# Agent attention and feed-forward: source order on four engines inside the main loop, and the attention work spread over single steps

## The chip, the cores and the metric

The kernel runs on one core of one Trainium2 chip. The metric is the device time of one launch in microseconds (us), the median of several executions. The core has five engines that run side by side and meet only at semaphores: PE (matrix multiplication; its weight loads are shown as PEld), DVE (elementwise work and reductions), ACT (activation functions and copies), POOL (elementwise work in SBUF) and SP, which here only issues DMAs. Each engine runs its own instructions in the order in which the program lists them.

## The reference, cut to what matters

```python
B, N, C, A = 4, 12480, 128, 49          # batches, tokens, width, agents
def sm(a, b):
    s = scale * (a @ b.transpose(0, 2, 1))
    s = s - s.max(-1, keepdims=True)
    e = np.exp(s)
    return e / (e.sum(-1, keepdims=True) + 1e-09)
agent_v = sm(agents, k) @ v             # per batch, 49 x 128
attn    = sm(q, agents) @ agent_v       # per batch, 12480 x 128
h = attn.reshape(49920, 128) @ w_in     # to 2048 hidden values
out = (h / (1 + np.exp(-1.702 * h))) @ w_out
```

A batch's queries need the sums over all of that batch's keys and values. All is float32 in the reference; `w_in` and `w_out` come as float64.

## The kernel before, in words

**Tiling.** A group is 960 tokens; a batch has 13 groups, and there are 52 in all. The 2048 hidden values of a group are computed in 16 steps of 128, so the main loop (L540 to L569) has 832 steps. `agent_v` is never multiplied with the query weights by itself: it is first multiplied into `w_in` (L306), once a batch, and the product is kept as a high part `wh` and a low part `wl` in float32r (L307, L308).

**A step.** `up` (L357) makes four matmuls of 128 x 480 columns into two of the four PSUM buffers `ph`, then ACT takes the gelu of both (L369, output `g`, three buffers), then `gh`, g rounded to float32r, is made on ACT (L371) for the steps listed in `HI_ON_ACT` and on DVE (L373) for the others, then DVE makes the rest `gl = g - gh` (L374). Both have `LAG + 1` = 5 buffers. `down` (L377) of the step four earlier makes six matmuls into the group's output `po`. After a group's last `down`, `store` copies `po` on ACT (L396) and SP sends it.

**Beside it**, for the next group: the query load (SP), `split` of the queries into three bfloat16 parts (POOL, L167 to L169), 32 small matmuls for the scores with the agents (`scores`, L182 to L185, two of the two PSUM buffers `ps_m`) whose two banks DVE reduces (L189), the softmax (DVE max and subtraction, L321 and L322; ACT exp, L328; DVE sum, reciprocal and product, L330 to L334), and four transposes with two ACT copies and two DVE subtractions that give the pairs `sa`, `sb` on which the next group's `up` works (L345 to L353).

**For the next batch**, spread over the 13 groups of this one: 13 key chunks in groups 0 to 5 (1 to 5 in batch 0): load, `split` on POOL, the same 32 matmuls, two reductions and a maximum (L225). Then `key_max` (L229): a DVE maximum, a PE transpose (L235), two DVE instructions, a second transpose (L241), a DVE copy. Then 13 value chunks in groups 6 to 11: the shift by the maximum on POOL (L251), exp on ACT (L255), the high and low parts of the weights on ACT and POOL (L260, L261) and of the values on DVE (L267, L268), eight matmuls (L272), and the sum on DVE (L287). In group 12 `agent_weights` (L289) makes `wh` and `wl` for the next batch. In batch 0's group 0, steps 1, 5 and 9, there is `down_weights` (L142) besides: eight DVE instructions that turn a quarter of `w_out` from float64 words to float32 (`to_float32`, L124 to L136), an ACT copy (L145) and a DVE subtraction (L146). The words, the keys and the values share three buffers `kv`; `rest` of `split` and the temporary of `to_float32` share two.

**What sets the order.** The source puts these jobs at steps of the group (`beside`, L509, and the constants of L27 to L35): at a step, jobs first, then `up`, then `down`. The source's order isn't the program's: the framework's scheduler puts the instructions of every engine in an order of its own. It works through them by priority (earlier source first) against modelled times, and where one isn't ready it takes a later one. So one engine's order can leave the source's order, matmul by matmul. Once it is compiled the order is fixed.

Of the kernel before, what the change touches and what calls it, by code (L numbers as in the profile page):

```python
# [27 lines left out]
E_AT = 4  # L28
S_AT = 0
V_AT = 7  # L30
VP = 2
VS = 4
P_AT = 12
QS_AT = 11
K_AT = 5  # L35
FIRST_WORDS = (1, 3, 5, 7)
FIRST_UP = (0, 2, 4, 6)
HI_ON_ACT = (0, 2, 4, 6, 8, 10, 12, 14)
# [4 lines left out]
def kernel(  # L43
# [36 lines left out]
    # sel[k, m] = 1 where k and m name the same agent in either half  # L80
# [28 lines left out]
    # a float64's words, low then high, to the nearest float32; what is under  # L109
    # float32's range becomes zero and what is over it infinite  # L110
# [5 lines left out]
    def to_float32(w, out=None):  # L116
# [4 lines left out]
        # 2 ** exponent, with the sign  # L121
# [6 lines left out]
        # the mantissa's upper 45 bits as a whole number, rounded once  # L128
# [19 lines left out]
    # ---- scores: a float32 is the sum of three bfloat16, and of the parts'  # L148
    # products all are summed but those under a float32 product's own rounding ----
# [13 lines left out]
    # the upper half of a word is the first part; of what is left the upper  # L163
    # half is the second, and the third takes the place of the lower
# [35 lines left out]
    def first_key_scores(g, kt):  # L200
        # two batches' agents to a pass, as many columns as keep the clock up
# [20 lines left out]
    def key_scores(b, g, parts):  # L222
        s = score[:TB, g * KB : (g + 1) * KB, :]
        scores(b, parts, s)
        nc.vector.tensor_reduce(  # L225
            out=part_max[:TB, g, :], in_=s.rearrange("p j a -> p a j"), axis=AX.X, op=ALU.max
        )

    def key_max():  # L229
# [3 lines left out]
        )  # L233
        ps = ps_m.tile([P, 512], F32, name="ps_m")
# [4 lines left out]
        nc.vector.tensor_copy(out=mrow[:A], in_=mcol[:A].broadcast_to([A, TB]))  # L239
        ps = ps_m.tile([P, 512], F32, name="ps_m")  # L240
        nc.tensor.transpose(out=ps[:TB, :A], in_=mrow[:A], identity=ident[:A, :A])  # L241
        nc.vector.tensor_copy(out=max_b[:TB], in_=ps[:TB, :A])

# [19 lines left out]
    def value_pair(g, vt, hi_copy, parts=1):  # L263
        vp = v_pair[g % 2]
        n = KB // parts
        for s in [slice(i * n, (i + 1) * n) for i in range(parts)]:
            hi_copy(out=vp[:TB, s, 0:C], in_=vt[:TB, s])  # L267
            nc.vector.tensor_sub(out=vp[:TB, s, C : 2 * C], in0=vt[:TB, s], in1=vp[:TB, s, 0:C].bitcast(F32))  # L268
# [11 lines left out]
    def key_values(g, vt, acc):  # L280
        value_pair(g, vt, nc.vector.tensor_copy)
        ps = ps_m.tile([P, 512], F32, name="ps_m")
        key_matmuls(g, ps, True, True)
        if g == 0:
# [4 lines left out]
    def agent_weights(acc):  # L289
        ps = ps_m.tile([P, 512], F32, name="ps_m")  # L290
        nc.tensor.matmul(out=ps[:, 0:P], lhsT=acc[:, 0:C], rhs=sel, start=True, stop=False)
        nc.tensor.matmul(out=ps[:, 0:P], lhsT=acc[:, C : 2 * C], rhs=sel, start=False, stop=True)
        zc = work.tile([P, P], F32, name="zc", bufs=1)
        nc.vector.tensor_copy(out=zc, in_=acc[:, 2 * C : 2 * C + 1].broadcast_to([P, P]))
# [6 lines left out]
        wh = wpool.tile([P, F], F32R, name="wh")  # L301
        wl = wpool.tile([P, F], F32R, name="wl")
        for c in range(F // 512):
            s = slice(c * 512, (c + 1) * 512)
            pw = ps_m.tile([P, 512], F32, name="ps_m")
            nc.tensor.matmul(out=pw, lhsT=avT, rhs=w_in_sb[:, s], start=True, stop=True)  # L306
            nc.scalar.copy(out=wh[:, s], in_=pw)  # L307
            nc.vector.tensor_sub(out=wl[:, s], in0=pw, in1=wh[:, s].bitcast(F32))  # L308
        return wh, wl

# [6 lines left out]
    def query_shift(b, parts):  # L317
        sd = work.tile([P, KB, A], F32, name="sd", bufs=SD)
        scores(b, parts, sd[:TB])
        m = work.tile([P, KB], F32, name="m")  # L320
# [4 lines left out]
        return sd  # L325

    def query_softmax(g, e):
        nc.scalar.activation(out=e[:TB], in_=e[:TB], func=AF.Exp, scale=scale)  # L328
        z = work.tile([P, KB], F32, name="z")
        nc.vector.tensor_reduce(out=z[:TB], in_=e[:TB], axis=AX.X, op=ALU.add)  # L330
        nc.vector.tensor_scalar_add(out=z[:TB], in0=z[:TB], scalar1=EPS)
        nc.vector.reciprocal(out=z[:TB], in_=z[:TB])
        pp = p_pad[g % 2]
# [23 lines left out]
    def up(f, wts, pairs):  # L357
# [7 lines left out]
        g = gpool.tile([P, 2, CH], F32, name="g")  # L365
        gh = gpool.tile([P, 2, CH], F32R, name="gh", bufs=LAG + 1)
        gl = gpool.tile([P, 2, CH], F32R, name="gl", bufs=LAG + 1)
        for c in range(2):
            nc.scalar.activation(out=g[:, c, :], in_=ph[c][:, :CH], func=AF.Gelu_apprx_sigmoid)  # L369
# [36 lines left out]
    shifted = {}  # L406
# [26 lines left out]
    def do_key_values(b, g):  # L433
        if g == 0:
            accs[b] = work.tile([P, 2 * C + 1], F32, name="acc")
        key_values(g, vts.pop((b, g)), accs[b])

    def do_query_scores(n):
        if n < B * NG:
            b, g = divmod(n, NG)  # L440
            shifted[n] = query_shift(b, q_parts.pop(n))

    def do_query_softmax(n):
        if n < B * NG:
            query_softmax(n, shifted.pop(n))
# [5 lines left out]
    def do_weights(b):  # L451
        wts[b] = agent_weights(accs.pop(b))
# [28 lines left out]
    do_query_scores(0)  # L481
    do_query_softmax(0)
# [22 lines left out]
    do_weights(0)  # L505
    down_weights(0, words[0])

    # what is done for the next batch beside a group: in steps of the group's
    def beside(b, g):  # L509
        jobs = {}  # L510
        if b == 0 and g == 0:
            for i in range(1, NF // 4):
                jobs.setdefault(4 * i - 3, []).append(lambda i=i: down_weights(i, words[i]))
        if b + 1 < B:
            late = 1 if b == 0 else 0
            ks = [k for k in range(NKG) if late + k * (6 - late) // NKG == g]
            vs = [k for k in range(NKG) if k * 6 // NKG == g - 6]
            for i, k in enumerate(ks):
                jobs.setdefault(0, []).append(lambda k=k: do_key_load(b + 1, k))
                jobs.setdefault(4 * i, []).append(lambda k=k: do_key_split(b + 1, k))  # L520
                jobs.setdefault(K_AT + 4 * i, []).append(lambda k=k: do_key_scores(b + 1, k))
            if g == 5:
                jobs.setdefault(15, []).append(key_max)
            if vs:
                assert S_AT < E_AT < V_AT - VP
                jobs.setdefault(E_AT, []).append(lambda: key_exp(vs[0], len(vs)))
            for i, k in enumerate(vs):
                jobs.setdefault(0, []).append(lambda k=k: do_value_load(b + 1, k))
                jobs.setdefault(S_AT, []).append(lambda k=k: key_shift(k, nc.gpsimd.tensor_tensor))
                jobs.setdefault(V_AT - VP + VS * i, []).append(lambda k=k: key_pair(k))  # L530
                jobs.setdefault(V_AT + VS * i, []).append(lambda k=k: do_key_values(b + 1, k))
            if g == NG - 1:
                jobs.setdefault(2, []).append(lambda: do_weights(b + 1))
        assert all(f < NF for f in jobs)
        return jobs

    steps = B * NG * NF
    live = {}
    po = {}
    for t in range(steps + LAG):  # L540
        n, f = divmod(t, NF)
        if t < steps:
            b, g = divmod(n, NG)
            if f == 0:
                jobs = beside(b, g)
            if f == 0:
                do_query_load(n + 2)
                if n == 0:
                    do_query_split(1)
            if f == QS_AT:  # L550
                do_query_split(n + 2)
            if f == Q_AT:
                do_query_scores(n + 1)
            if f == E_AT:
                do_query_softmax(n + 1)
            for job in jobs.get(f, ()):
                job()
            if f == P_AT:
                do_query_pairs(n + 1)
            live[t] = up(f, wts[b], pairs[n])  # L560
            if f == NF - 1:
                pairs.pop(n)
        if t >= LAG:
            n, f = divmod(t - LAG, NF)
            if f == 0:
                po[n] = [ps_o.tile([P, 512], F32, name=f"po{c}") for c in range(2)]
            down(f, live.pop(t - LAG), po[n])
            if f == NF - 1:
                store(*divmod(n, NG), po.pop(n))  # L569
# [38 lines left out]
```

## Time and profile before

| | us |
|---|---|
| median of 3 runs (lowest, highest) | 2137.14 (2136.03, 2139.71) |
| the profiled execution, span from first to last instruction | 2139.6 |
| first matmul of the main loop | 73.00 |
| start of group 13, of group 26, of group 39 (batches 1, 2, 3) | 610.75, 1133.19, 1654.86 |
| mean granted TensorE clock | 0.992 of full speed |

The execution that was profiled is thus 2.5 us over the median; what lies outside its span isn't shown. The profile's page gives the busy time of each engine. A matmul's end is modelled and matmuls overlap, so PE busy isn't PE at its peak; it shows where PE had nothing to do. The windows view gives the same in stretches of time that one chooses: length, then busy us of each engine with the number of instructions, then the share of the clock that was granted to TensorE. The waits view says which engine's instruction ended the waits of another.

### The profile page before, as it was taken

The page shows a single profiled execution, that of the slowest core. Times are in us where ns is not written, and L with a number is a line of the kernel's source. Part 1 is how long each engine was busy: PE and PEld are TensorE (multiplying, and loading weights), DVE is VectorE, ACT ScalarE, POOL GpSimd, SP SyncE. Part 2 cuts the span into 40 slices and gives each one's busy share as a digit, 9 for nine tenths or more (in the row PEclk, how much of TensorE's full clock was granted, in tenths as well). Part 3 has the DMA queues.
Part 4 walks back from the last instruction along what each step waited for, and adds up shares of the span by engine and source line. Part 5 has one row for each costly group of instructions (what it writes and reads, how often), then busy time and mean ns, then how long its engine had stood idle before and what let it go on. Part 6 is the DMA issues. An engine that isn't in the chain of part 4 may idle for free.

```text
span 2139.6 us, 31613 instructions
## 1 busy us (share of the span) xinstructions
PE 2083.2 (97%) x12232; PEld 1777.1 (83%) x12232; DVE 1865.0 (87%) x2142; ACT 1611.9 (75%) x2590; POOL 519.8 (24%) x383
## 2 busy tenths in 40 slices
PE   8889989999999999999999999999999999999999
PEld 8678878888888887788888888778888888888887
DVE  6998998999889899899888899899898887888876
ACT  3567768977777776987777777798777877778786
POOL 4143445121123433421113342531110101001000
PEclk9999999999999999999999999999999999999999
DMA  9411221211111212112101212111100101010000
GB/s 265 119 48 49 65 73 38 61 48 50 38 38 47 66 47 56 47 56 56 56 20 47 63 49 56 55 51 53 47 19 19 38 19 38 19 38 20 25 14 19
DMA packets 49339, 108.57 MB, mean 51 GB/s; under 512 B 4252, under 2 KB 30172, under 8 KB 49188
## 3 DMA queue, kind: packets, MB, share of 16 engines
q1 hardware_dynamic: 49188, 106.55, 17.2%
q8 instruction: 96, 1.57, 0.3%
q14 instruction: 55, 0.45, 0.1%
HBM read 80.97 MB, written 25.56 MB: 50 GB/s over the span
## 4 chain that ended last, share of the span: by engine, by line
PE 81%; DVE 11%; issue 3%; ACT 3%; POOL 1%; DMA 1%; ACTq 0%; SPq 0%; DVEq 0%; POOLq 0%
PE po L385 43%; PE ph L362 15%; PE ph L364 14%; DVE gl L374 5%; DVE gh L373 2%; PE ps_m L272 1%; PE ps_m L182 1%; PE ps_m L184 1%; POOL score L251 1%; PE ps_m L205 1%; ACT g L369 1%; PE ps_m L345 1%; PE ps_m L306 1%; PE ps_m L183 1%; PE ps_m L185 1%
## 5 line engine op out<-in xcount | busy, mean ns | idle before, releaser
L374 DVE TENSOR_TENSOR gl<-g,gh 128x960 fp32r<-128x960 f32 x832 | 1034.4, 1258 | 189.4 <-ACT gh L371 174.3
L369 ACT ACTIVATE g<-ph 128x480 f32<-128x480 f32 x1664 | 855.2, 573 | 380.5 <-PE ph L364 265.7
L385 PE MATMUL po<-gl,wo_h 128*128 128x480 f32 x1664 | 501.9, 382 | 5.4 <-DVE gl L374 5.4
L385 PE MATMUL po<-gh,wo_h 128*128 128x480 f32 x1664 | 506.1, 383 | 0.7 <-ACT gh L371 0.7
L385 PE MATMUL po<-gh,wo_l 128*128 128x480 f32 x1664 | 501.6, 383 | 0.0
L371 ACT CAST gh<-g 128x960 fp32r<-128x960 f32 x416 | 416.0, 1000 | 10.9
L385 PEld LDWEIGHTS po<-gl,wo_h 128*128 128x128 f32 x1664 | 313.1, 189 | 60.0 <-DVE gl L374 9.2
L385 PEld LDWEIGHTS po<-gh,wo_h 128*128 128x128 f32 x1664 | 313.5, 189 | 53.2 <-ACT gh L371 1.1
L385 PEld LDWEIGHTS po<-gh,wo_l 128*128 128x128 f32 x1664 | 313.8, 189 | 49.9
L362 PE MATMUL ph<-sa,wh 128*128 128x480 f32 x832 | 332.5, 400 | 4.8 <-ACT g L369 4.8
L364 PE MATMUL ph<-sa,wl 128*128 128x480 f32 x832 | 319.3, 384 | 0.0
L362 PE MATMUL ph<-sb,wh 128*128 128x480 f32 x832 | 318.8, 383 | 0.0
L364 PE MATMUL ph<-sb,wl 128*128 128x480 f32 x832 | 316.6, 381 | 0.0
L373 DVE CAST gh<-g 128x960 fp32r<-128x960 f32 x416 | 298.6, 718 | 7.0 <-ACT g L369 6.6
L167 POOL MEMSET qt<- 128x8 f32 x52 | 5.7, 110 | 939.2 <-PE ps_m L185 472.0
L169 POOL TENSOR_TENSOR rest<-rest 128x968 bf16<-128x968 f32 x91 | 188.6, 2072 | 7.1
L362 PEld LDWEIGHTS ph<-sa,wh 128*128 128x128 f32 x832 | 157.7, 190 | 31.7 <-ACT g L369 10.8
L362 PEld LDWEIGHTS ph<-sb,wh 128*128 128x128 f32 x832 | 158.0, 190 | 26.6 <-ACT g L369 6.2
L364 PEld LDWEIGHTS ph<-sb,wl 128*128 128x128 f32 x832 | 156.9, 189 | 25.6 <-issue 1.0
L364 PEld LDWEIGHTS ph<-sa,wl 128*128 128x128 f32 x832 | 157.1, 189 | 24.7 <-issue 1.0
L168 POOL TENSOR_TENSOR rest<-qt 128x968 f32<-128x968 f32 x52 | 110.7, 2129 | 167.8 <-DMA qt<-qT 110.8
L184 PE MATMUL ps_m<-ag_part,rest 128*128 128x98 bf16 x728 | 110.2, 205 | 0.0
(103 smaller groups left out, 2077.8 us busy)
## 6 DMA issues: line engine op xcount, KB each, us to landing
kt<-kT SPq DMA_DIRECT2D x52, 480.0 KB, 3.6
qt<-qT SPq DMA_DIRECT2D x52, 480.0 KB, 3.8
vt<-v SPq DMA_DIRECT2D x52, 480.0 KB, 4.3
outT<-o SPq DMA_DIRECT2D x104, 240.0 KB, 2.2
words<-w_in SPq DMA_DIRECT2D x4, 512.0 KB, 10.9
words<-w_out SPq DMA_DIRECT2D x4, 512.0 KB, 8.2
ag_sb<-agT SPq DMA_DIRECT2D x1, 98.0 KB, 2.1
```

The source lines that it names most:

```text
L168: nc.gpsimd.tensor_sub(out=r, in0=t, in1=halves(t)[0])
L169: nc.gpsimd.tensor_sub(out=halves(r)[1], in0=r, in1=halves(r)[0])
L182: mm(out=o, lhsT=x0[:, t], rhs=a[:, 0 : 2 * A], start=True, stop=False)
L183: mm(out=o[:, A:], lhsT=x0[:, t], rhs=a[:, 2 * A :], start=False, stop=False)
L184: mm(out=o, lhsT=x1[:, t], rhs=a[:, 0 : 2 * A], start=False, stop=False)
L362: nc.tensor.matmul(out=ph[c][:, :CH], lhsT=wh[:, s], rhs=pairs[c], start=True, stop=False)
L364: nc.tensor.matmul(out=ph[c][:, :CH], lhsT=wl[:, s], rhs=pairs[c], start=False, stop=True)
L369: nc.scalar.activation(out=g[:, c, :], in_=ph[c][:, :CH], func=AF.Gelu_apprx_sigmoid)
L371: nc.scalar.copy(out=gh, in_=g)
L373: nc.vector.tensor_copy(out=gh, in_=g)
L374: nc.vector.tensor_sub(out=gl, in0=g, in1=gh.bitcast(F32))
L385: nc.tensor.matmul(out=po[c][:, :CH], lhsT=lhsT[:, f, :], rhs=rhs[:, c, :], start=(f == 0 and first), stop=(f == NF - 1 and last),)
```

## The change

Four things are done together.

1. The loop stands in `tc.manual_schedule(engines={PE, Activation, DVE, Pool})`: inside it these four engines take their instructions in the order of the source. SP isn't among them.
2. A step's order in the source becomes `up` with its two gelus, then the step's jobs, then `gh` and `gl` (the new `high_low`), then `down` of four steps earlier. Before, the jobs stood ahead of `up`, and `gh` and `gl` were part of it.
3. The jobs are cut into pieces, and each has a step. `key_scores` loses its maximum (`key_part_max`, a step later), `key_max` becomes three pieces (DVE; a transpose and two DVE instructions; a transpose and a DVE copy), `key_values` becomes the values' high part and low part, the matmuls, and the sum, at two steps before, one before, the step, and one after. The softmax is cut into shift, exp, sums and product. `agent_weights` becomes `weights_sums` and four `weights_part`, a step each. Steps on which PE has a job are given out by `pe_step`, which takes the next step that has none; each group's steps 4 (query scores) and 13 (query pairs) are taken from the start. Key chunks stand 6 steps apart in batch 0 (from step 16 of the batch) and 7 in the others (from step 6), value chunks 7 apart.
4. Constants: the exp of the queries moves from step 4 to step 7, and the key chunks' exps are put straight behind it, up to three chunks in one instruction, so that both use the exp table while it is loaded. The pairs move from step 12 to 13, the query split from 11 to 14, the query load from 0 to 5. `HI_ON_ACT` still has eight steps of 16, with 5 and 13 in place of 4 and 8.

The work is otherwise the same: each engine has the same instructions on the same operands, apart from the exps that are put together. The diff, cut to its core:

```diff
-E_AT = 4
-P_AT = 12
-QS_AT = 11
+E_AT = 7
+P_AT = 13
+S_AT = 14
-HI_ON_ACT = (0, 2, 4, 6, 8, 10, 12, 14)
+HI_ON_ACT = (0, 2, 5, 6, 10, 12, 13, 14)
...
+    for i in range(1, NF // 4):
+        put(4 * i - 3, lambda i=i: down_weights(i, words[i]))
+    put(0, lambda: do_query_split(1))
+    for b in range(B - 1):
+        s0 = b * per_batch
+        first, apart = (16, 6) if b == 0 else (6, 7)
+        for k in range(NKG):
+            t = pe_step(s0 + first + apart * k)
+            put(max(t - 13, s0), lambda b=b, k=k: do_key_load(b + 1, k))
+            put(max(t - 6, s0), lambda b=b, k=k: do_key_split(b + 1, k))
+            put(t, lambda b=b, k=k: do_key_scores(b + 1, k))
+            put(t + 1, lambda k=k: key_part_max(k))
+        mx = {}
+        put(t + 2, lambda mx=mx: key_max_0(mx))
+        t = pe_step(t + 3)
+        put(t, lambda mx=mx: key_max_1(mx))
+        t = pe_step(t + 2)
+        put(t, lambda mx=mx: key_max_2(mx))
+        shift = t + 2
+        slot = next(t for t in range(shift + 3, steps) if t % NF == E_AT)
+        t = slot + 3
+        for k in range(NKG):
+            t = pe_step(t)
+            while t > slot + NF + 5:
+                slot += NF
+            exps.setdefault(slot, []).append(k)
+            put(min(shift + 3 * k, slot - 1), lambda k=k: key_shift(k, nc.gpsimd.tensor_tensor))
+            put(t - 14, lambda b=b, k=k: do_value_load(b + 1, k))
+            put(t - 2, lambda k=k: key_pair(k))
+            put(t - 2, lambda b=b, k=k: value_hi(k, vts[b + 1, k]))
+            put(t - 1, lambda b=b, k=k: value_lo(k, vts.pop((b + 1, k))))
+            put(t, lambda b=b, k=k: do_key_values(b + 1, k))
+            put(t + 1, lambda b=b, k=k: do_key_sum(b + 1, k))
+            last, t = t, t + 7
+        put(pe_step(last + 2), lambda b=b, w=w: weights_sums(accs.pop(b + 1), w))
+        t = last + 3
+        for c in range(F // 512):
+            t = pe_step(t + 1)
+            put(t, lambda b=b, w=w, c=c: weights_part(b + 1, w, c))
+    for n in range(B * NG):
+        s0 = n * NF
+        put(s0 + Q_AT, lambda n=n: do_query_scores(n + 1))
+        put(s0 + Q_AT + 1, lambda n=n: do_query_load(n + 2))
+        put(s0 + Q_AT + 1, lambda n=n: do_query_shift(n + 1))
+        put(s0 + E_AT, lambda n=n: do_query_exp(n + 1))
+        if s0 + E_AT in exps:
+            put(s0 + E_AT, lambda ks=ks: key_exp(ks[0], len(ks)))
+        put(s0 + E_AT + 2, lambda n=n: do_query_sums(n + 1))
+        put(s0 + E_AT + 3, lambda n=n: do_query_softmax(n + 1))
+        put(s0 + P_AT, lambda n=n: do_query_pairs(n + 1))
+        put(s0 + S_AT, lambda n=n: do_query_split(n + 2))
...
+    with tc.manual_schedule(engines={E.PE, E.Activation, E.DVE, E.Pool}):
+        for t in range(steps + LAG):
+            if t < steps:
+                n, f = divmod(t, NF)
+                g = up(f, wts[n // NG], pairs[n])
...
+            for job in at.pop(t, ()):
+                job()
+            if t < steps:
+                live[t] = high_low(f, g)
+            if t >= LAG:
...
+                down(f, live.pop(t - LAG), po[n])
```

More of the change, by code (lines that the diff above doesn't have):

```diff
@@ L227, in key_scores, with key_max_0 @@
         )
-    def key_max():
+    def key_max_0(d):
         mx = work.tile([P, A], F32, name="mx", bufs=1)
@@ L239, in key_max, with key_max_2 @@
         nc.vector.tensor_copy(out=mrow[:A], in_=mcol[:A].broadcast_to([A, TB]))
+        d["mrow"] = mrow
+    def key_max_2(d):
+        mrow = d["mrow"]
         ps = ps_m.tile([P, 512], F32, name="ps_m")
@@ L242, in key_max @@
         nc.vector.tensor_copy(out=max_b[:TB], in_=ps[:TB, :A])
+    def key_max():
+        d = {}
+        key_max_0(d)
+        key_max_1(d)
+        key_max_2(d)
     def value_load(b, g):
@@ L261, in key_pair, with value_hi, value_lo @@
         nc.gpsimd.tensor_sub(out=ep[:TB, :, H : H + A], in0=sc, in1=ep[:TB, :, 0:A].bitcast(F32))
-    def value_pair(g, vt, hi_copy, parts=1):
+    def value_hi(g, vt):
+        nc.vector.tensor_copy(out=v_pair[g % 2][:TB, :, 0:C], in_=vt[:TB])
+    def value_lo(g, vt):
         vp = v_pair[g % 2]
[L265 to L268, printed above, removed]
+        nc.vector.tensor_sub(out=vp[:TB, :, C : 2 * C], in0=vt[:TB], in1=vp[:TB, :, 0:C].bitcast(F32))
     def key_matmuls(g, ps, first, last):
@@ L300, in agent_weights, with weights_part @@
         nc.vector.tensor_mul(out=avT, in0=ps[:, 0:P], in1=rz)
[L301 to L309, printed above, removed]
+        w["avT"] = avT
+    def weights_part(b, w, c):
+        if c == 0:
+            wts[b] = wpool.tile([P, F], F32R, name="wh"), wpool.tile([P, F], F32R, name="wl")
+        wh, wl = wts[b]
+        s = slice(c * 512, (c + 1) * 512)
+        pw = ps_m.tile([P, 512], F32, name="ps_m")
+        nc.tensor.matmul(out=pw, lhsT=w["avT"], rhs=w_in_sb[:, s], start=True, stop=True)
+        nc.scalar.copy(out=wh[:, s], in_=pw)
+        nc.vector.tensor_sub(out=wl[:, s], in0=pw, in1=wh[:, s].bitcast(F32))
     def query_load(b, g):
@@ L315, in query_load, with query_scores, query_shift @@
         return t
-    def query_shift(b, parts):
+    def query_scores(b, parts):
         sd = work.tile([P, KB, A], F32, name="sd", bufs=SD)
         scores(b, parts, sd[:TB])
+        return sd
+    def query_shift(sd):
         m = work.tile([P, KB], F32, name="m")
@@ L365, in up, with high_low @@
         g = gpool.tile([P, 2, CH], F32, name="g")
+        for c in range(2):
+            nc.scalar.activation(out=g[:, c, :], in_=ph[c][:, :CH], func=AF.Gelu_apprx_sigmoid)
+        return g
+    def high_low(f, g):
         gh = gpool.tile([P, 2, CH], F32R, name="gh", bufs=LAG + 1)
         gl = gpool.tile([P, 2, CH], F32R, name="gl", bufs=LAG + 1)
-        for c in range(2):
-            nc.scalar.activation(out=g[:, c, :], in_=ph[c][:, :CH], func=AF.Gelu_apprx_sigmoid)
         if f in HI_ON_ACT:
@@ L405 @@
     q_parts = {}
-    shifted = {}
+    scored = {}
+    sums = {}
     accs = {}
@@ L504 @@
     do_query_load(1)
-    do_weights(0)
+    w0 = {}
+    weights_sums(accs.pop(0), w0)
+    for c in range(F // 512):
+        weights_part(0, w0, c)
     down_weights(0, words[0])
[L509 to L535, printed above, removed]
@@ L538 @@
+    E = mybir.EngineType
     live = {}
     po = {}
[L540 to L556, printed above, removed]
-                job()
[L558 to L569, printed above, removed]
+    with tc.manual_schedule(engines={E.PE, E.Activation, E.DVE, E.Pool}):
[3 more added lines that the diff above has]
+                g = up(f, wts[n // NG], pairs[n])
+                if f == NF - 1:
+                    pairs.pop(n)
+            for job in at.pop(t, ()):
+                job()
+            if t < steps:
+                live[t] = high_low(f, g)
+            if t >= LAG:
+                n, f = divmod(t - LAG, NF)
+                if f == 0:
+                    po[n] = [ps_o.tile([P, 512], F32, name=f"po{c}") for c in range(2)]
+                down(f, live.pop(t - LAG), po[n])
+                if f == NF - 1:
+                    store(*divmod(n, NG), po.pop(n))
@@ L573 @@
+    assert not at
 _INS = ["qT", "kT", "v", "agT", "w_in", "w_out"]
```

64 lines of the change are left out of this document (47 added, 17 removed).

## The prediction

> **What bounds the kernel now.** I read the page first, then the windows by batch and by group, then PE's waits.
>
> ```profile
> span 2139.6 us, 31613 instructions
> PE 2083.2 (97%) x12232; PEld 1777.1 (83%) x12232; DVE 1865.0 (87%) x2142; ACT 1611.9 (75%) x2590; POOL 519.8 (24%) x383
> ```
>
> PE has work for 97% of the span. The windows by batch are cut at the first `up` matmul of groups 0, 13, 26, 39 and 51 (columns: length, then busy us of PE, PEld, DVE, ACT, POOL, then the granted clock):
>
> ```profile
> core 0: us, PE busy (x) PEld busy (x) DVE busy (x) ACT busy (x) POOL busy (x), PEclk, DMA share, GB/s
> 73.00:610.75 537.75, 517.72 (x3067) 437.38 (x3065) 488.77 (x561) 407.44 (x649) 157.60 (x109) 0.99 0.17 50
> 610.75:1133.19 522.44, 514.42 (x3085) 438.43 (x3084) 471.17 (x533) 404.17 (x644) 148.25 (x104) 0.99 0.17 50
> 1133.19:1654.86 521.67, 513.45 (x3086) 438.10 (x3085) 470.33 (x533) 404.43 (x644) 150.29 (x101) 1.00 0.16 47
> 1654.86:2095.03 440.17, 440.17 (x2353) 376.00 (x2352) 359.49 (x409) 350.25 (x564) 37.58 (x30) 1.00 0.08 25
> ```
>
> In the last row PE never stops: twelve groups with query work alone take 440.17, so 36.68 each. That is PE's own pace, and no order can beat it. Now single groups, cut the same way:
>
> ```profile
> 73.00:113.00 40.00, 36.15 (x194) 28.21 (x193) 39.27 (x59) 30.00 (x49) 11.99 (x8) 0.98 0.17 50
> 113.00:161.58 48.58, 42.58 (x278) 34.87 (x276) 47.23 (x48) 31.13 (x51) 18.60 (x13) 0.96 0.18 52
> 161.58:203.48 41.90, 40.43 (x293) 34.70 (x292) 38.15 (x43) 29.54 (x47) 18.25 (x12) 1.00 0.20 60
> 492.45:531.00 38.55, 38.55 (x214) 33.47 (x213) 35.74 (x43) 30.18 (x49) 6.90 (x7) 1.00 0.17 51
> 569.60:610.75 41.15, 41.15 (x212) 33.25 (x210) 34.39 (x42) 31.67 (x51) 3.90 (x3) 1.00 0.08 25
> 652.78:691.82 39.04, 39.04 (x261) 33.56 (x260) 35.91 (x42) 29.43 (x47) 13.52 (x9) 1.00 0.17 51
> 808.99:853.30 44.31, 40.89 (x263) 34.48 (x262) 43.69 (x50) 29.73 (x49) 15.10 (x9) 0.95 0.20 56
> 853.30:897.74 44.44, 41.93 (x221) 35.20 (x220) 37.42 (x39) 38.16 (x58) 25.95 (x19) 0.97 0.17 45
> ```
>
> Three of these also run without a PE gap and give the price of the jobs to PE: two key chunks 39.04 - 36.68, so 1.18 each; two value chunks 38.55 - 36.68, so 0.94 each; the weights 41.15 - 36.68 = 4.47. A batch that prepares the next one therefore costs PE at least 13 x 36.68 + 13 x 1.18 + 13 x 0.94 + 4.47, and about 0.3 for the two transposes of `key_max` (an estimate by the 0.30 of a row below): 509.2. The three batches took 537.75, 522.44 and 521.67: **28.6, 13.2 and 12.5 too much, 54.3 in all**. This is what another order can win. It sits in few groups. In batch 1: `key_max` (808.99, two chunks: 44.31 against 39.3) and the first value group (853.30, three chunks: 44.44 against 39.5) hold ten of the 13.2. Batch 0 has the like, and group 1 (113.00, three chunks: 48.58 against 40.2), 8.4 over. The waits of PE, summed over the run, name who is late:
>
> ```profile
> PE ps_m L182 <- DVE sb L353: 10.2, 5, 3.9
> PE ps_m L241 <- DVE mrow L239: 7.6, 3, 3.5
> PE po L385 <- DVE gl L374: 5.4, 9, 2.1
> PE ph L362 <- ACT g L369: 4.8, 6, 1.6
> PE ps_m L182 <- DVE sd L189: 4.5, 2, 4.2
> PE ps_m L272 <- POOL e_pair L261: 3.2, 2, 2.2
> 850.50 0.30 PE L241 MATMUL ps_m<-ident,mrow 49*120 49x49 f32 x1 [3.42 <-DVE mrow L239]
> 853.30 0.60 PE L362 MATMUL ph<-sa,wh 128*128 128x480 f32 x1
> L362 PE MATMUL ph<-sb,wh 128*128 128x480 f32 x832 | 318.8, 383 | 0.0
> ```
>
> Scores follow pairs or other scores at once and find their `ps_m` buffer not yet emptied (L182, 14.7). The second transpose of `key_max` stands where DVE can't be done yet (L241, 7.6). The last three rows, two of the timeline and one of the groups by line, show what such a wait also costs: after 3.42 us of idleness a matmul takes 0.60 that takes 0.383 on average, as PE's clock is down for a while. That explains the 0.95 granted in that window.
>
> **The change part by part.** (1) *A step for each PE job.* Scores, pairs, value matmuls, transposes and weights now stand at least a step, 2.2 us, apart (36.68 less the scores' 1.18 and some 0.4 for transposes, over 16). The buffer that a job needs is then emptied by instructions that DVE has in its queue at or near the step of the job before. I take the L182 waits and the half-clock stretches behind them as gone. What is late next: in batch 0 the first transpose of `key_max` is one step after the maximum and not two, because the last chunk is at step 88. There the maximum (L231) stands behind a step with sums on DVE; I estimate 1.4 of wait, about one such instruction:
>
> ```profile
> L231 DVE TENSOR_REDUCE mx<-part_max 120x49 f32<-120x637 f32 x4 | 5.3, 1314 | 0.0
> L374 DVE TENSOR_TENSOR gl<-g,gh 128x960 fp32r<-128x960 f32 x832 | 1034.4, 1258 | 189.4 <-ACT gh L371 174.3
> L369 ACT ACTIVATE g<-ph 128x480 f32<-128x480 f32 x1664 | 855.2, 573 | 380.5 <-PE ph L364 265.7
> L371 ACT CAST gh<-g 128x960 fp32r<-128x960 f32 x416 | 416.0, 1000 | 10.9
> L373 DVE CAST gh<-g 128x960 fp32r<-128x960 f32 x416 | 298.6, 718 | 7.0 <-ACT g L369 6.6
> ```
>
> In each batch `weights_sums` has a PE matmul that needs `zc`, and DVE's copy of it stands behind the `gl` of the step before: 0.9 (below one `gl`). (2) *Source order.* Between `up` of a step and the end of its `gl` lie two gelus (1.03 back to back), `gh` 0.72 to 1.00, `gl` 1.26: about 3.2 us. The third next gelu needs that `g` buffer, 6.6 after the first, and `ph` gives two steps more. So DVE may be 3 us late without ACT noticing, and ACT some 2 more without PE noticing. The heaviest stretch that I find is a value chunk on step 10 of a group: DVE has on steps 8 to 11 the values' two parts, the sums, the product and the accumulation besides; added up, DVE is 2 to 3 us behind and comes back by step 14. This is inside the allowance, so I cost it at nothing; if DVE were 3 us later still, each such stretch would stop PE by the excess. (3) *The exp at step 7.*
>
> ```profile
> 1510.91 1.28 ACT L328 ACT_TABLE_LOAD   x1
> 1512.20 0.53 ACT L328 ACTIVATE sd<-sd 120x392 f32<-120x392 f32 x1
> 1512.75 1.28 ACT L369 ACT_TABLE_LOAD   x1
> 1514.05 1.96 ACT L369 ACTIVATE g<-ph 128x480 f32<-128x480 f32 x4
> ```
>
> The block takes 1514.05 - 1510.91 = 3.14. The gelu of step 8 is queued behind it and ends 1.03 + 3.14 + 1.03 = 5.2 after `up` of step 7; `up` of step 10 needs that buffer 5.7 to 5.9 after. Margin 0.6. With key chunks in the block 0.5 to 1.2 is added, so I charge 0.3 in each of six groups a batch, 1.8. Fewer table loads in all help ACT, which isn't late. [...]
>
> (4) *Group 0.* Here the order costs something new:
>
> ```profile
> L132 DVE TENSOR_SCALAR tmp<-words 128x512 uint32<-128x512 uint32 x8 | 3.6, 446 | 0.0
> L136 DVE SCALAR_TENSOR_TENSOR m<-m,tmp 128x512 f32<-128x512 f32 x4 | 3.7, 925 | 0.0
> L145 ACT CAST wo_h<-m 128x512 fp32r<-128x512 f32 x4 | 2.5, 623 | 18.7 <-DVE m L136 18.7
> L146 DVE TENSOR_TENSOR wo_l<-m,wo_h 128x512 fp32r<-128x512 f32 x4 | 4.4, 1088 | 0.3 <-ACT wo_h L145 0.3
> ```
>
> `down_weights` is eight DVE instructions between 0.45 and 0.93, so 3.6 to 7.4, which I take at 4.5, then the cast on ACT, 0.6, then 1.1 on DVE. In source order the cast stands on ACT ahead of the next step's gelu: gelu(2), gelu(6) and gelu(10) wait until DVE has converted. Today DVE mixes conversion and `gl`, and ACT passes over the cast. At step 1 PE has only up(2) and up(3) left to do and stops for some 5 us, and pays 1.5 for the clock. At steps 5 and 9 it has two `up` and two or three `down`, about 4.4 of cover, against a cast that is late by 4.5 and by DVE's own delay from the scores: 2 and 3 us of stop. The exp block behind step 5's cast adds 1.5. With 1 us for filling the pipeline that is 14 over 36.68, so about 51 for group 0, against 40.00 today. Bounds: 40 (PE lives on the buffers as it does today) and 58 (each of three conversions fully exposed, 7).
>
> **The sum**, over the 509.2 of a batch. Batch 0: 14 (group 0) + 1.4 + 0.9 + 1.8 = 18.1, of 28.6. Batches 1 and 2: 0.9 + 1.8 and about 1.8 for waits that I can't place, 4.5 each, of 13.2 and 12.5. Batch 3 stays. Won: 10.5 + 8.7 + 8.0 = 27.2, so 2139.6 - 27.2 = 2112.4 for a profiled execution like this one, and 2.5 less for a median like 2137.1: **2110**.
>
> **The rivals.** *A, group 0 hides its conversions and nothing else is left.* For it: today's group 0 has the same work and only 3.3 too much. Against it: the cast holds ACT. Time: 2137.1 - 54.3 + 3.3 + 9.5 (the waits of (1) to (3): 4.1, 2.7 and 2.7) = 2096, between 2088 and 2100.
>
> *B, half of it comes back in small waits.* Group 0 near its upper bound (7 more) and 3 more us in each batch, as DVE is busy for 38.15 of a group of 40.2 with three key chunks, 95%, and an order that can't be left wastes some of the rest: 2110 + 16 = 2126, between 2120 and 2140.
>
> *C, slower: DVE becomes the bound.* DVE's largest wait is `gl` for ACT's `gh`: 174.3 us, 0.42 for each of the 416 steps that have it, eight a group. Today other DVE work is pulled into such holes; in strict order what stands behind `gl` waits with it. A value group has 35.74 of DVE work in 38.55, so 2.8 to spare. The rival decides where the holes exceed this while DVE is late: at 0.35 a step. At 0.5 a step they are 4.0, 1.2 too much, in 36 groups 43: 2110 + 43 = 2153. Against it: a hole opens only where DVE is ahead, and the change puts the jobs on steps 5, 6, 10, 12 to 14, where `gh` is on ACT, ahead of `gl`, that is into the hole. Strongest sign for it: DVE at 43.69 of 44.31 in the `key_max` group.
>
> [...]
>
> **How the numbers follow.** The forecast has 0.52 (its own range 2100 to 2120), A 0.16, B 0.15, C 0.15, D 0.02. A measurement of this kernel can tell 0.2%, 4.3 us, from no change: under 2132.9 is faster, over 2141.4 slower. B is split, 0.09 faster, 0.05 within, 0.01 over. So faster 0.52 + 0.16 + 0.09 = 0.77, same 0.05, slower 0.15 + 0.02 + 0.01 = 0.18. The range from 2093 to 2144 leaves out D, all of C but its mildest quarter (0.11), and the lower third of A (0.05): 0.18.
>
> **What would show it.** In the profile after: groups 1 to 12 of each batch at their PE price (39.0 with two key chunks, 38.6 with two value chunks), no L182 row with `sb` or `sd` in PE's waits, the `key_max` transposes without a wait but for about 1.4 in batch 0; group 0 near 51, with ACT's cast waiting on DVE and PE's `ph` on `g`; exp loads down to about two a group. It is wrong if query groups of batch 3 leave 36.68, which would be the exp at step 7, or if key and value groups settle above their price by the same amount each, which would be C, with DVE idle before `gl` well over 174.3.

## The result, and the profile after

The changed kernel takes 2272.65 us, median of 4 runs (2271.37 to 2277.8); the kernel before takes 2136.68 in the runs beside it. The ratio is 1.0635, interval 1.062 to 1.065: clearly slower, where the prediction had 2110 and a range from 2093 to 2144.

The page of the changed kernel, first line and busy times:

```profile
span 2271.6 us, 31765 instructions
PE 2126.4 (94%) x12232; PEld 1810.4 (80%) x12232; DVE 1918.7 (84%) x2142; ACT 1578.6 (69%) x2560; POOL 530.3 (23%) x383
```

No engine became the bound. All five rows show a smaller busy share than before, DVE too (84% against 87%). The span grew by 132.0 us, and something is waited for. The windows by batch of the changed kernel, cut as before at the first `up` matmul of groups 0, 13, 26, 39 (length; busy us of PE, PEld, DVE, ACT, POOL; granted clock):

```profile
74.24:664.45 590.21, 533.76 (x3066) 448.10 (x3065) 508.09 (x561) 395.72 (x639) 154.30 (x108) 0.96 0.15 46
664.45:1227.44 562.99, 528.38 (x3086) 448.55 (x3084) 487.56 (x533) 392.75 (x634) 151.68 (x104) 0.97 0.16 46
1227.44:1787.45 560.01, 525.35 (x3085) 446.59 (x3084) 486.00 (x533) 392.77 (x634) 152.35 (x103) 0.98 0.15 44
1787.45:2227.05 439.60, 439.60 (x2354) 377.94 (x2352) 362.75 (x409) 351.76 (x564) 45.91 (x30) 1.00 0.08 26
```

The loss lies in the three batches that prepare another: 52.5, 40.6 and 38.3 us over the kernel before. Batch 3, with query work alone, has even gained 0.6. Within a batch the windows by group of the changed kernel separate key groups from value groups:

```profile
74.24:127.42 53.18, 40.10 (x179) 29.88 (x178) 45.24 (x62) 30.75 (x50) 8.05 (x7) 0.91 0.13 37
703.80:742.78 38.98, 38.98 (x261) 33.53 (x260) 37.09 (x40) 29.31 (x47) 14.74 (x11) 1.00 0.17 51
861.37:900.52 39.15, 39.15 (x262) 33.62 (x261) 35.84 (x44) 29.30 (x47) 8.70 (x5) 1.00 0.19 51
996.13:1044.12 47.99, 42.94 (x213) 36.03 (x212) 35.61 (x40) 31.00 (x50) 9.00 (x6) 0.91 0.14 41
1044.12:1092.88 48.76, 42.06 (x213) 35.55 (x212) 36.41 (x41) 30.53 (x50) 5.88 (x5) 0.89 0.14 41
```

The second and third rows, key groups 14 and 18 of batch 1, run at PE's own pace without a gap. That is what the prediction wanted (group 18, where `key_max` begins, took 44.31 before). The last two are value groups 21 and 22, 48 to 49 us against the 38.55 that two chunks need. In them DVE has 36 us of work and stands idle for 12. PE's waits in the changed kernel name the cause at once:

```profile
PE ps_m L284 <- DVE v_pair L280: 100.7, 36, 6.5
PE ph L386 <- ACT g L391: 10.9, 7, 4.6
PE ps_m L369 <- DVE score L184: 6.2, 2, 4.7
PE ps_m L237 <- DVE mx L229: 4.4, 2, 2.7
PE ps_m L310 <- DVE zc L307: 1.9, 3, 0.6
```

And the groups by line show DVE's two largest (busy us, mean ns, idle us ahead of them and what ended it):

```profile
L401 DVE TENSOR_TENSOR gl<-g,gh 128x960 fp32r<-128x960 f32 x832 | 1096.2, 1323 | 179.7 <-ACT gh L398 162.0 <-PE ph L388 1.4
L400 DVE CAST gh<-g 128x960 fp32r<-128x960 f32 x416 | 334.8, 805 | 74.0 <-ACT g L391 73.4
```

The value matmuls (L284) wait for the values' low part (L280, `value_lo`): 100.7 us in 36 of 39 chunks, a row that the kernel before doesn't have. The longest of these waits, in the timeline of the changed kernel, DVE, then POOL, then PE (start, length, engine):

```profile
506.30 0.66 DVE L400 CAST gh<-g 128x960 fp32r<-128x960 f32 x1 [3.09 <-ACT g L391]
...
509.82 2.22 DVE L400 CAST gh<-g 128x960 fp32r<-128x960 f32 x1
512.07 2.63 DVE L401 TENSOR_TENSOR gl<-g,gh 128x960 fp32r<-128x960 f32 x1
514.63 0.68 DVE L276 CAST v_pair<-vt 120x1024 fp32r<-120x1024 f32 x1
515.23 0.55 DVE L358 TENSOR_TENSOR p_pad<-sd,z 120x392 f32<-120x392 f32 x1
515.71 1.14 DVE L401 TENSOR_TENSOR gl<-g,gh 128x960 fp32r<-128x960 f32 x1
516.78 1.21 DVE L280 TENSOR_TENSOR v_pair<-vt,v_pair 120x1024 fp32r<-120x1024 f32 x1
509.72 1.80 POOL L163 TENSOR_TENSOR rest<-qt 128x968 f32<-128x968 f32 x1
511.60 2.10 POOL L164 TENSOR_TENSOR rest<-rest 128x968 bf16<-128x968 f32 x1
511.24 0.38 PE L388 MATMUL ph<-sb,wl 128*128 128x480 f32 x1
518.13 2.06 PE L284 MATMUL ps_m<-v_pair,e_pair 120*128 120x258 f32 x8 [6.51 <-DVE v_pair L280]
519.99 1.00 PE L412 MATMUL po<-gh,wo_h 128*128 128x480 f32 x2
```

PE ends `up` of the step at 511.6 and its next job is the value matmuls. The chunk is on step 12 of group 9, and DVE has the low part in its queue one step before; but ahead of it stand `gh` and `gl` of the steps up to 10, held up by the gelu behind the exp (3.09 us idle at 506.30) and then drawn out to 2.22 and 2.63 us while POOL splits queries. Nothing may pass, so the low part starts at 516.78 and PE goes on at 518.13. Behind the wait PE runs slower: the eight matmuls show 2.06, and the granted clock is 0.50 from 518.13 to 523.50.

### The profile page after: what moved, and what is told of

Read it like the earlier page. It is cut to its first block, busy times and chain, and to the rows that moved or that the text cites. A ratio compares the mean times of both kernels' runs of the same rounds, so it can differ in the third digit from the quotient of the medians.

```text
span 2271.6 us, 31765 instructions
## 1 busy us (share of the span) xinstructions
PE 2126.4 (94%) x12232; PEld 1810.4 (80%) x12232; DVE 1918.7 (84%) x2142; ACT 1578.6 (69%) x2560; POOL 530.3 (23%) x383
## 4 chain that ended last, share of the span: by engine, by line
PE 75%; DVE 16%; ACT 5%; issue 3%; DMA 1%; POOL 0%; ACTq 0%; SPq 0%; DVEq 0%; POOLq 0%
PE po L412 40%; PE ph L386 13%; PE ph L388 13%; DVE gl L401 6%; DVE v_pair L280 3%; PE ps_m L284 3%; DVE gh L400 3%; ACT g L391 2%; ACT gh L398 1%; PE ps_m L177 1%; PE ps_m L200 1%; PE ps_m L179 1%; PE ps_m L369 1%; PE ps_m L324 1%; PE ps_m L178 1%
## 5 line engine op out<-in xcount | busy, mean ns | idle before, releaser
L401 DVE TENSOR_TENSOR gl<-g,gh 128x960 fp32r<-128x960 f32 x832 | 1096.2, 1323 | 179.7 <-ACT gh L398 162.0
L412 PE MATMUL po<-gh,wo_h 128*128 128x480 f32 x1664 | 525.9, 398 | 0.0
L400 DVE CAST gh<-g 128x960 fp32r<-128x960 f32 x416 | 334.8, 805 | 74.0 <-ACT g L391 73.4
L412 PEld LDWEIGHTS po<-gl,wo_h 128*128 128x128 f32 x1664 | 319.6, 192 | 52.6
L412 PEld LDWEIGHTS po<-gh,wo_h 128*128 128x128 f32 x1664 | 304.9, 193 | 44.8 <-issue 5.7
L386 PE MATMUL ph<-sa,wh 128*128 128x480 f32 x832 | 321.2, 386 | 10.6 <-ACT g L391 10.5
L164 POOL TENSOR_TENSOR rest<-rest 128x968 bf16<-128x968 f32 x91 | 215.8, 2372 | 7.1
L273 POOL TENSOR_TENSOR e_pair<-score,e_pair 120x392 fp32r<-120x392 f32 x39 | 42.1, 1079 | 640.8 <-ACT e_pair L272 591.2
L163 POOL TENSOR_TENSOR rest<-kt 128x968 f32<-128x968 f32 x39 | 78.5, 2013 | 375.8 <-issue 360.5
L284 PE MATMUL ps_m<-v_pair,e_pair 120*128 120x258 f32 x312 | 60.3, 350 | 101.2 <-DVE v_pair L280 100.7
```

The lines of the kernel that those rows point to most:

```text
L163: nc.gpsimd.tensor_sub(out=r, in0=t, in1=halves(t)[0])
L164: nc.gpsimd.tensor_sub(out=halves(r)[1], in0=r, in1=halves(r)[0])
L273: nc.gpsimd.tensor_sub(out=ep[:TB, :, H : H + A], in0=sc, in1=ep[:TB, :, 0:A].bitcast(F32))
L284: nc.tensor.matmul(out=ps[:, : 2 * C + 2], lhsT=e_pair[g % 2][:TB, j, :], rhs=v_pair[g % 2][:TB, j, :], start=(first and j == 0), stop=(la ...
L386: nc.tensor.matmul(out=ph[c][:, :CH], lhsT=wh[:, s], rhs=pairs[c], start=True, stop=False)
L400: nc.vector.tensor_copy(out=gh, in_=g)
```

## The experiments

Three theories. **Theory 1**: in source order DVE reaches a step's jobs a step and more after PE does, so data that DVE makes one step ahead of a PE job can't be there in time; the lead is too short, and no instruction may pass another to repair it. **Theory 2** (the prediction's rival C): DVE has no room for strict order, and its holes bound the kernel. **Theory 3**: source order on POOL puts the query split on the very stretch in which DVE works towards the low part. Every ratio is against the kernel before, timed beside each run. Differences in us are between medians that were not all timed together; the kernel before itself lay between 2136.68 and 2141.54, so they can be some 5 us off.

**e1: two steps more lead.**

```diff
-            put(t - 2, lambda b=b, k=k: value_hi(k, vts[b + 1, k]))
-            put(t - 1, lambda b=b, k=k: value_lo(k, vts.pop((b + 1, k))))
+            put(t - 4, lambda b=b, k=k: value_hi(k, vts[b + 1, k]))
+            put(t - 3, lambda b=b, k=k: value_lo(k, vts.pop((b + 1, k))))
```

> The changed kernel with the values' high part put 4 and the low part 3 steps ahead of the value matmuls (before 2 and 1); all else as changed. Theory 1 (the lead is too short: DVE reaches a step's jobs more than a step after PE, and PE waits 100.7 us for the values' low part): these waits go, and with them the half-clock stretches; batches 1 and 2 fall from 563 and 560 to 510 to 520, the median from 2273 to 2115 to 2140. Theory 2 (strict order leaves DVE without room): PE's waits move to the gelus' buffers or to gl, value groups stay over 43 us, the median stays over 2200. Theory 3 (source order on POOL puts the query split on the very gh and gl that stand ahead of the low part): the collisions stay, with two steps more lead they are hidden, so the time is that of theory 1, but gh and gl keep their stretched means of 0.81 and 1.32.

Measured: 2162.52, ratio 1.0103 (1.0087 to 1.012). The waits on the low part are gone, all of them, and with them 110 us. The value groups of batch 1, in the windows of this kernel:

```profile
942.08:983.11 41.03, 39.49 (x214) 33.12 (x212) 38.40 (x40) 30.54 (x50) 14.74 (x9) 1.00 0.17 49
983.11:1023.98 40.87, 39.50 (x213) 33.27 (x214) 37.09 (x43) 29.19 (x49) 7.39 (x5) 1.00 0.18 49
1104.05:1151.54 47.49, 43.39 (x211) 35.42 (x210) 39.51 (x44) 31.47 (x51) 9.63 (x8) 0.93 0.07 22
```

Value groups fell from 48 to 41; theory 2, which wanted over 43 and over 2200, falls with its number. The means of `gh` and `gl` stay at 0.82 and 1.35, as theory 3 said: the collisions with POOL are still there, and the lead hides them. But 2162 is above theory 1's 2115 to 2140: the last row, the group that makes the weights, rose to 47.49 from 41.6, because its sums wait for the last accumulation, put one step ahead as well:

```profile
PE ps_m L308 <- DVE acc L301: 12.1, 3, 4.1
```

In the changed kernel this wait was hidden: PE had just stood for the values, and DVE had caught up.

**e4: one step more.** The same edit with 3 and 2 steps.

> The same with one step more lead alone (high part 3, low part 2 steps ahead). Theory 1: one step is 2.2 us; of the waits listed (36, mean 2.8, longest 6.5) each loses up to 2.2, so some 70 of 100.7 us go, and the median comes to about 2160 to 2190. Theory 2: as in the other, over 2200.

Measured: 2183.45, ratio 1.0202 (1.0185 to 1.0218), and 22.5 us of waits on the low part in 12 chunks. So 100.7, 22.5, 0 with 1, 2, 3 steps of lead. The second step took 78 us, 2.2 from each of the 36 waits on the mean, which is the length of a step, as theory 1 has it.

**e2: POOL left out of source order.**

```diff
-    with tc.manual_schedule(engines={E.PE, E.Activation, E.DVE, E.Pool}):
+    with tc.manual_schedule(engines={E.PE, E.Activation, E.DVE}):
```

> The changed kernel with POOL left out of the engines that keep source order; the lead stays one step. Theory 3: the splits no longer start right behind the weights' low part, the stretch of gh and gl ahead of the values goes, and the waits on the low part fall from 100.7 to under 50 us: 2180 to 2220. Theory 1 alone: DVE's own order is what makes the low part late, waits stay within 85 to 115 us: 2255 to 2285.

Measured: 2246.85, ratio 1.0495 (1.0479 to 1.0512), waits on the low part 80.7. It lies between the two expectations. POOL's order is a minor part, 26 us (31 by the ratios); the splits met other `gl` instead (mean of `gl` 1.338 us, 1.323 as changed).

**e3: nothing held to source order.** The block above without its engines: the new steps and pieces, the scheduler's order.

> The changed source with its new steps and pieces, but no engine held to source order: the scheduler orders all, as in the kernel before. If the steps themselves are poor, it is slow too, over 2200. If holding to source order is what costs (theories 1 to 3), the scheduler slips the values' parts ahead and it comes to 2110 to 2150.

Measured: 2156.87, ratio 1.0072 (1.0057 to 1.0087), no wait on the low part. A little over the expected range: the new steps by themselves are 0.7% slower than the old ones, and 116 us of the loss come with the order.

**e8: the query split's work left out.** Two POOL subtractions become one memset, from the third group on; the queries' second and third parts are zero in it.

```diff
+        if free:
+            nc.gpsimd.memset(r, 0.0)
+        else:
-        nc.gpsimd.tensor_sub(out=r, in0=t, in1=halves(t)[0])
-        nc.gpsimd.tensor_sub(out=halves(r)[1], in0=r, in1=halves(r)[0])
+            nc.gpsimd.tensor_sub(out=r, in0=t, in1=halves(t)[0])
+            nc.gpsimd.tensor_sub(out=halves(r)[1], in0=r, in1=halves(r)[0])
```

> The changed kernel as it was timed (values' low part one step ahead), but POOL's two subtractions for the queries are left out from the third group on and one memset put in their place, so the queries' second and third parts are zero and that part of the scores isn't computed. Everything else, the matmuls too, is there. Theory 3 (POOL's split on the same stretch as DVE's gh and gl makes the low part late): the waits on the low part fall from 100.7 to under 60, gl's mean from 1.32 to under 1.25, the time to 2195 to 2225. Theory 1 alone: within 20 us of 2272.

Measured: 2216.19, ratio 1.0352 (1.0332 to 1.0373). The groups by line and PE's waits of this kernel:

```profile
L404 DVE TENSOR_TENSOR gl<-g,gh 128x960 fp32r<-128x960 f32 x832 | 1023.0, 1233 | 200.2 <-ACT gh L401 182.5 <-PE ph L391 1.4
PE ps_m L287 <- DVE v_pair L283: 69.6, 36, 4.3
```

The time lies in theory 3's range, and so does the mean of `gl` (1.233); theory 1 alone, within 20 us of 2272, is refuted. But the waits fall by 31 us, not by the 41 that theory 3 asked for, and still 36 chunks wait. The collisions with POOL make DVE later, and without them the lead is too short just the same: both theories hold, one for the lead, one for part of the lateness.

**e11: DVE alone left out of source order.**

```diff
-    with tc.manual_schedule(engines={E.PE, E.Activation, E.DVE, E.Pool}):
+    with tc.manual_schedule(engines={E.PE, E.Activation, E.Pool}):
```

> The changed kernel as it was timed, with DVE alone left out of the engines that keep source order (steps, leads, PE, ACT and POOL as changed). Theory 1 (DVE's strict order behind a short lead): the scheduler can pull the values' parts ahead of gh and gl on DVE, the waits on the low part fall from 100.7 to under 40, the time to 2150 to 2200. If the step given to PE's job is itself too early for the data whatever DVE's order: over 2240.

Measured: 2141.61, ratio 1.0004 (0.9994 to 1.0015): **the whole loss is gone**, 131 us, more than expected. By line and tile POOL's order is that of the changed kernel, and PE's and ACT's differ in the first step of the loop alone; what differs is where DVE does what. The timeline of this kernel at the chunk that waited longest, step 12 of group 9:

```profile
463.15 0.68 DVE L276 CAST v_pair<-vt 120x1024 fp32r<-120x1024 f32 x1
464.82 1.22 DVE L280 TENSOR_TENSOR v_pair<-vt,v_pair 120x1024 fp32r<-120x1024 f32 x1
477.79 1.13 PE L284 MATMUL ps_m<-v_pair,e_pair 120*128 120x258 f32 x8
```

The scheduler started the low part 13.0 us ahead of its matmuls, where source order had it 1.35 ahead, and the eight matmuls take 1.13 in place of 2.06. The windows of groups 0 and 1 and of value groups 21 and 22 in this kernel:

```profile
73.95:117.59 43.64, 38.29 (x178) 26.75 (x177) 42.90 (x60) 29.89 (x49) 9.94 (x7) 0.99 0.16 46
117.59:166.40 48.81, 43.52 (x292) 36.78 (x293) 45.33 (x46) 31.77 (x51) 17.57 (x12) 0.93 0.17 51
933.15:972.26 39.11, 39.09 (x213) 33.34 (x212) 36.45 (x43) 30.93 (x50) 12.77 (x9) 1.00 0.18 51
972.26:1011.04 38.78, 38.78 (x214) 33.30 (x212) 35.64 (x40) 30.49 (x50) 7.18 (x5) 1.00 0.18 52
```

With about the same DVE work as in the changed kernel, 36.45 and 35.64 against 35.61 and 36.41, the value groups are near 38.55 again.

**e5, e6, e7, e9, e10: what else a short lead costs, with DVE held.** Each adds to the one before, from e1 on. e5: the weights' sums and parts two steps later.

```diff
-        put(pe_step(last + 2), lambda b=b, w=w: weights_sums(accs.pop(b + 1), w))
-        t = last + 3
+        put(pe_step(last + 4), lambda b=b, w=w: weights_sums(accs.pop(b + 1), w))
+        t = last + 5
```

> The kernel with two more steps of lead for the values, and the sums for the weights (and with them the four parts) two steps later as well: four steps behind the last value chunk and not two. There PE waits 4.0 us three times for the accumulation that DVE has queued one step before, and the groups that make the weights take 47.0 to 47.5 us. Theory 1 (DVE reaches a step's work a step and more after PE): these groups fall to 41.2 to 42.5, the median by 14 to 18 us from 2162.5, to about 2147. Theory 2 (DVE has no room): the wait moves behind, the median stays over 2156.

Measured: 2158.63 (1.0069 to 1.0099 of before), 4 us and not 14 to 18: a miss for theory 1, and by its number the branch of theory 2. The wait for the accumulation went, but the next one stood behind it, PE for `zc`, which DVE makes on the very step on which PE needs it: 9.8 us in 3 waits, where it had been 0.5 in e1 and 1.9 in the changed kernel. Here the lead is not even a step; whether it is lead or room that is short stays open until e12.

e6: the conversion of `w_out` in four pieces.

```diff
-        put(4 * i - 3, lambda i=i: down_weights(i, words[i]))
+        put(4 * i - 3, lambda i=i, d=d: words_exponent(words[i], d))
+        put(4 * i - 2, lambda i=i, d=d: words_mantissa(words[i], d))
+        put(4 * i, lambda i=i, d=d: words_high(i, d))
+        put(4 * i + 1, lambda i=i, d=d: words_low(i, d))
```

> The same, and the conversion of w_out in group 0 cut in four: four DVE instructions at steps 1, 5 and 9, four a step later, ACT's cast three steps later and DVE's subtraction four steps later. The prediction's account of group 0 (ACT's cast holds the next gelu until DVE has converted) gives 42 to 46 us for group 0, in place of 53, so 7 to 11 us less than without, about 2138. If group 0 is slow because DVE has too much to do there, its 53 stay within 3 us.

Measured: 2162.44 (1.0084 to 1.0117), no gain. PE's waits on the gelu, 10.8, fell to 2.5, but group 0 came down from 55.0 (e5) to 50.6 only and group 1 rose from 42.1 to 47.5; the transposes now wait up to 5.4 for the softmax's product. The cast in ACT's queue isn't all that makes group 0 slow: with it out of the way DVE is late for PE there by other ways.

e7: no key scores on steps 3 and 12, and the first transpose of `key_max` a step later.

```diff
-            t = pe_step(s0 + first + apart * k)
+            t = s0 + first + apart * k
+            while t % NF in (Q_AT - 1, P_AT - 1) or t in pe_steps:
+                t += 1
+            pe_steps.add(t)
...
-        t = pe_step(t + 3)
+        t = pe_step(t + 4)
```

> The same again, and no key scores on the step right ahead of the query scores or pairs (steps 3 and 12 of a group are passed over for keys), and the first transpose of the key maximum one step later. PE waits there for 6.2 us on a score buffer that DVE has not reduced (4.8 at 284 us, behind scores at step 12) and for 4.4 on the maximum in batch 0. Theory 1: the two go, groups 1 and 5 fall from 42.1 and 47.6 to about 40.5 and 40.0, the median by another 8 to 11, to about 2129, under the kernel before.

Measured: 2146.28 (1.0019 to 1.0043), 16 us less, more than expected: groups 1, 4 and 5 fell from 47.5, 47.6 and 41.5 to 42.7, 41.8 and 39.6 (the group with the wait at 284 us is group 4, not 5). Not yet under the kernel before.

e9: `zc` in a step of its own.

```diff
+        put(last + 1, lambda b=b, w=w: weights_zc(accs[b + 1], w))
         put(pe_step(last + 4), lambda b=b, w=w: weights_sums(accs.pop(b + 1), w))
```

> The last kernel with DVE's copy of the weights' sum (zc) in a step of its own, three steps ahead of the PE matmul that needs it and no longer on the same step. PE waits there three times 3.3 us, and runs at half clock behind. Theory 1: the groups that make the weights fall from 44.2 to 46.7 to about 41.5, the median by 11 to 15 from 2146.3, to 2131 to 2135. Theory 2: it stays within 3 us of 2146.

Measured: 2145.12 (1.0013 to 1.0032), 1 us and not 11 to 15: a second miss of the same kind, and within the 3 us of theory 2's branch. The wait for `zc` is gone, and in its place the query scores, one step behind, wait 5.8 for the buffer that the sums still hold.

e10: in group 0 ACT makes `gh` on all steps but 7 and 8.

```diff
-        if f in HI_ON_ACT:
+        if f in HI_ON_ACT or (first and f not in (7, 8)):
```

> The same, and in group 0 alone ACT makes gh on all steps but 7 and 8, so that DVE has 6 copies less there. Group 0 takes 50.6 with DVE at 45 busy while ACT has 30, and PE waits 5.4 for the softmax's product behind the conversions. If DVE's amount of work bounds group 0: 44 to 48 and 2126 to 2130. If the order is what costs there, no change within 2 us.

Measured: 2139.46, ratio 0.9992 (0.9982 to 1.0001), as fast as before, but not the 2126 to 2130 of the expectation. Group 0 fell to 47.8 and group 1 to 41.1, 4.3 us together, of 5.7 in the median; so half a dozen copies less on DVE help there.

**e12: both remedies.** e10 with DVE left out of source order.

> The two remedies together: all the longer leads and group 0's changes, and DVE left out of the engines that keep source order. With DVE held the same leads gave 2139.5, with DVE free and the short leads 2141.6; what is left in the two lies in different groups (held: 0.3 to 1.5 us in each value group and 3 in the weights' group; free: 6 us in the first value group of a batch and 8 in group 1). If what is left of both is a short lead somewhere, the two add up: 2110 to 2130, under the kernel before. If what is left is DVE's amount of work, 95% of a group, they don't: 2133 to 2142.

Measured: **2127.0, ratio 0.9945 (0.9931 to 0.9959)**: they add up, as the expectation has it for short leads and not for the amount of DVE's work, and the version beats both kernels, the one before by half a percent. Group 0 takes 40.55. PE's waits in it:

```profile
PE ps_m L210 <- DVE sd L217: 8.0, 2, 4.1
PE ps_m L210 <- DVE avT L352: 5.3, 3, 1.8
```

What is left, 6 us in the `key_max` group of a batch (group 18, 45.75, which the expectation takes for the first value group) and 1.5 in the weights' group, wasn't tried.

## Why the prediction was wrong

Taken in its own order:

- **PE's floor: right.** 36.68 for a query group stands (36.63 in all of batch 3), and so do the prices of key and value chunks (38.98 in group 14, 38.78 in group 22 with DVE free).
- **(1) A step for each PE job: right for buffers, wrong for data.** Of the L182 waits (14.7), scores that find their buffer full, 0.6 is left in the changed kernel; pairs right behind scores still wait 6.2 for theirs (L369), which e7 took away. It went wrong in the sentence that a job's buffer is emptied by instructions that DVE has "in its queue at or near the step of the job before": it asked what a job needs freed, and not what it needs made. `value_lo` is made for the value matmuls, one step ahead.
- **(2) Source order: the step that failed.** The text worked out that DVE ends a step's `gl` some 3.2 us after `up`, a step and a half, and even found the stretch: a value chunk on step 10, DVE "2 to 3 us behind". Then it held this against the allowance of the `g` and `ph` buffers only and cost it "at nothing". With the same numbers the low part of one step ahead ends at 3.2 + 1.2 = 4.4 us after the `up` two steps back, when PE is ready for it at 2 x 2.2 = 4.4: no allowance at all, so DVE's lateness of 2 to 3 us goes to PE in full. Measured: 36 waits of 2.8 on the mean. e1, e4 and e11 show it from two sides, by a longer lead and by a free order.
- The waits are 100.7 us of the 132. In value groups 19 to 24 of batch 1 the total over PE's price is 53, of which 33.5 are these waits; most of the rest is the granted clock, which is 0.89 to 0.96 in these groups. The prediction had quoted such a row, and priced it for group 0 alone.
- **`key_max` and `zc`**: the L237 row's 4.4 holds the 2.7 that stood ahead of the loop before the change as well, so 1.7 in batch 0 (1.4 was expected); `zc` 1.9 in three waits (0.9 each). Small, and right in kind.
- **(3) The exp at step 7: right for PE.** Batch 3 lost nothing, and all of PE's 10.9 us of waits for a gelu lie in group 0. Exp loads are 51, one a group, against 48 and 18 before. But the block holds up DVE as well, by 3.09 us ahead of the longest wait shown, and so has a part in the lateness of (2); how large a part wasn't tried.
- **(4) Group 0: right in size, and the cause that it names is only part of it.** 53.18 against 51, and the waits that it foretold are there: in group 0 ACT's cast waits 13.3 us for DVE, PE 10.9 for the gelus. The longest stop, put at 5 and 1.5 for the clock, was 4.6 with a granted clock of 0.50 for 5.4 us behind it. But e6 took the cast out of ACT's way and won nothing over groups 0 and 1. Six copies less on DVE (e10) took 4.3 us off the two. And with DVE free, all its work and the cast in their place (e11), group 0 takes 43.64, though group 1 then takes 48.81, with one wait of 4.6 of pairs right behind scores, as in e6. So DVE's strict order has a part in group 0's loss, and the amount of its work another; how they divide stays open.
- **Rival C** had the sign and not the mechanism. DVE didn't become the bound: its idle time ahead of `gl` for `gh`, the sign that the prediction named, fell from 174.3 to 162.0, and in value groups it stood idle for 12 of 48 us. Holes did open elsewhere, ahead of `gh` for the gelu, 6.6 us before and 73.4 now (55.6 in e1, where PE's stops for the low part are gone), but value groups of 41 in e1 leave DVE room for them. **Rival D** (0.02, slower): no run shows a cost of a table load besides its own row. In the timeline of the changed kernel a load takes 1.28 us, and the next instruction starts 0.02 after the load for the exp (1842.54 + 1.28, then 1843.84) and 0.01 after the one for the gelu (1844.39 + 1.28, then 1845.68); batch 3, with an exp and two table loads in each group, kept its pace, 36.63 a group.

That DVE's strict order with a one-step lead is the cause is shown. How the 131 us divide between DVE's own queue and POOL's collisions is shown only in part: e8 gives 56 us for the query splits, but it takes DVE's stretched time away in all groups, so this isn't their share of the waits alone.

## What to carry to other kernels

When a queue is put into source order, lay down for every hand-over between two engines the moment at which the producer's queue reaches it and the moment at which the consumer needs it; buffers that come free are only half of the hand-overs. An engine at the end of a chain (here `up`, gelu, `gh`, `gl`) is late against the engine at its start, here by some 3.2 us by the prediction's estimate and by 2 to 3 more in the stretch with a value chunk; its jobs for that engine need this lateness as lead, here three steps (no wait left in e1) and not one (100.7 us of waits). And holding the late engine to an order gains nothing that the leads don't give: with longer leads, PE, ACT and POOL in source order and DVE free, it was the fastest of these kernels (2127.0, against 2139.46 with DVE held).

## What the hardware showed

- **POOL's subtractions held DVE up until they ended, nearly always.** In the timeline of the changed kernel above, DVE's `gh`, 0.66 us alone (506.30), starts 0.10 us after POOL's subtraction and takes 2.22: it ends 0.52 after POOL's does (509.72 + 1.80 = 511.52; 509.82 + 2.22 = 512.04). The next `gl` and POOL's second subtraction repeat it, 514.70 against 513.70. Throughout the changed kernel, 48 of the 50 `gh` and all 97 `gl` that start while a subtraction of `split` runs end 0.5 to 0.6 and 1.0 us after it, however early they started. The other two `gh` took 0.61 and ended before the subtraction did. The delay is in the DVE instructions' own rows and not in idle time ahead of them, so here one engine held another up without a semaphore.
- **A wait of PE costs more than itself.** After the 6.51 us at 511.6 the matmuls start 0.40 apart from 519.99 on until 523.59, and 0.22 apart from 524.72 on; in the kernel before it was 0.40 from 851.30 until 855.70, behind 3.42 us. The granted clock is 0.50 in both stretches, and 1.00 from 524.72 to 530.00. In the changed kernel the 0.50 follows all 21 waits for the low part of 2.8 us or more, for some 3 to 6 us, and none of the 15 of 1.4 us or less: behind 2.79 us it lasts from 950.44 to 953.80, with 1.00 after, and behind 1.03 us (970.69) the clock stays 1.00.
- **A removed wait shows the one behind it.** The weights' group took 41.6 us in the changed kernel, 46.7 to 47.5 with the value waits gone (e1), 44.2 to 46.8 in e5 to e7 and 44.3 in e9, as one after the other the accumulation, `zc` and the sums' buffer became the last to come.
